# Moves between partitions, issued from two queues instead of one, in a fused attention and feed-forward kernel

## The chip, the core and the metric

The kernel runs on one core of a Trainium2 chip. The metric is the time of one execution on the device in microseconds (us), median of several runs. TensorE does matrix products, VectorE and ScalarE do elementwise work, GpSimd issues the loads here, and SyncE does nothing but issue transfers. Each engine takes its instructions in order. ScalarE can issue transfers as well, from the same in-order queue that holds its copies and exponentials.

## What is computed

The input is q, k and v of 8 batches, 8 heads, 576 positions and 64 features. Attention runs inside chunks of 64 positions; its output, 4608 tokens of 512 features, goes through a feed-forward part with a product in its middle:

```python
scores = scale * np.matmul(q_c, k_c.transpose(0, 1, 2, 4, 3))   # chunks of 64
attn = np.exp(scores - max) ; attn = attn / sum
x = np.matmul(attn, v_c)            # brought to [4608, 512]
a = x @ w1                          # [4608, 1024]
b = x @ w2
h = a * b @ w3
out = h @ w_out                     # [4608, 512], float32
```

The kernel works in bfloat16 with float32 accumulation and computes w3 @ w_out once, so that two products remain behind a * b.

## The kernel before

The whole schedule is a list of steps, ORDER, and each engine's instructions run in that order. The tokens are cut into 18 pairs of 256 tokens; two pairs form a group of 512. The letters that matter here:

- T transposes Q or K of a pair in blocks of 32 (VectorE). G moves the result of a group between partitions; S computes the scores (TensorE), E the exponential (ScalarE), P the product with V, N the normalisation (VectorE).
- X transposes the attention output (VectorE), H moves it between partitions.
- A and B are the two gate products of one slice (TensorE), C copies A's result from PSUM to SBUF (ScalarE), M multiplies it by B's (VectorE). A digit behind the dot is the slice; A8.4 is slice 4 of the group that begins with pair 8.
- O is the output product, Y its copy to SBUF (ScalarE), Q the store.

For pairs 0 to 7 neither G nor H is used: the scores are computed from blocks of 32 rows as they lie, and X writes the final layout. From pair 8 on, in groups 4 to 8, the 32-row blocks are moved so that scores need half as many matmuls. A move is a transfer from SBUF to SBUF, 32 partitions at a time.

```python
ps = ctx.enter_context(tc.tile_pool(name="ps", bufs=4, space=bass.MemoryType.PSUM))

def psum(name):                       # all PSUM tiles: four, in turn
    return ps.tile([P, 2, 512], f32, tag="p", name=name)

def move(dst, src):
    inorder(nc.sync.dma_start(dst, src))

def do_G(g, a):                       # a = 0 or 1: the two halves of the eight moves
    if a == 0:
        qkm_t[g] = asb.tile([P, 2, 2, 2, H, CH], bf, tag="qkm", bufs=2, name="qkm")
    for i in (0, 2, 1, 3):
        e = (i + a) % 2
        move(qkm_t[g][blk[i // 2 * 2 + e], i % 2], qkT_t[g][blk[i], e])

def do_H(g, a):
    xt = new_xt(g)[:].rearrange("p (s c) -> p s c", s=2)
    for i in (0, 2, 1, 3):
        move(xt[blk[i // 2 * 2 + a], i % 2], xm_t[g][blk[i], a].rearrange("p o m t -> p (o m t)"))

def do_C(p, j):
    a_t[p, j] = msb.tile([P, 512], f32, tag="a_sb", bufs=3, name="a_sb")
    inorder(nc.scalar.copy(a_t[p, j][:], ps_t[p, j][:, 0, :]))

def do_M(p, j):
    ...
    inorder(nc.vector.tensor_mul(o, view(a_t.pop((p, j))[:]), view(ps_t.pop((p, j))[:, 1, :])))

def store(p, u0, u1, n0, n1, o_sb):
    move(out[p * PT + u0 * UT:p * PT + u1 * UT, n0:n1].rearrange("(u p) n -> p u n", p=UT), o_sb)
```

Loads go through GpSimd's queue. The stretches of ORDER in which groups 5 and 6 are moved (cut):

```
... N8.0 A6.0 M4.7 B6.0 N8.1 C6.0 G5.1 A6.1 X8.0 B6.1 M6.0 C6.1 X8.1 P9 v15 q16 k16 A6.2 M6.1 ...
... C6.5 M6.4 A6.6 M6.5 B6.6 T12.1 H4.1 C6.6 S10 S11 M6.6 E10 A6.7 T13.0 B6.7 E11 P10 v16 q17 k17
T13.1 C6.7 O4 M6.7 G6.0 N10.0 N10.1 X10.0 G6.1 P11 v17 Y4 X10.1 O5 N11.0 N11.1 Q4 X11.0 X11.1 T14.0
A8.0 H5.0 Y5 B8.0 T14.1 C8.0 A8.1 M8.0 B8.1 H5.1 C8.1 T15.0 A8.2 B8.2 M8.1 C8.2 T15.1 Q5 A8.3 B8.3
C8.3 M8.2 G7.0 S12 M8.3 S13 E12 A8.4 T16.0 B8.4 E13 G7.1 P12 T16.1 C8.4 A8.5 B8.5 M8.4 ...
```

Of the kernel before, what the change touches and what calls it, by code (L numbers as in the profile page):

```python
# [7 lines left out]

ORDER = """
R0 R1 v0 q1 i0 k1 v1 i1 i2 q2 k2 v2 i3 q3 k3 v3 q4 k4 v4 o h0 h1 D0.0.16.64 K0 T0.0 K1 T0.1 q5 k5 v5  # L10
S0 T1.0 E0 P0 D0.1.4.512 T1.1 q6 k6 v6 N0.0 S1 D1.0.5.512 X0.0 N0.1 X0.1 A0.0 E1 B0.0 C0.0 P1 M0.0
A0.1 N1.0 X1.0 B0.1 C0.1 N1.1 A0.2 X1.1 B0.2 C0.2 M0.1 A1.0 T2.0 B1.0 C1.0 M0.2 A1.1 T2.1 q7 k7 v7
B1.1 C1.1 M1.0 S2 M1.1 A0.3 E2 T3.0 B0.3 C0.3 P2 M0.3 A1.2 N2.0 X2.0 B1.2 C1.2 N2.1 A1.3 X2.1 B1.3
C1.3 M1.2 A2.0 T3.1 q8 k8 v8 B2.0 C2.0 M1.3 S3 T4.0 A2.1 E3 M2.0 B2.1 T4.1 q9 k9 C2.1 P3 v9 M2.1
A2.2 N3.0 B2.2 C2.2 X3.0 A2.3 N3.1 B2.3 X3.1 C2.3 M2.2 S4 M2.3 A3.0 E4 B3.0 C3.0 A3.1 M3.0 B3.1 C3.1
V0 A3.2 M3.1 B3.2 C3.2 V1 A3.3 M3.2 B3.3 C3.3 V2 W0 M3.3 V3 W1 Z0 V4 V5 W2 Z1 V6 V7 T5.0 Z2 W3 T5.1
q10 k10 T6.0 T6.1 P4 v10 q11 k11 Z3 S5 N4.0 O0 E5 X4.0 N4.1 X4.1 T7.0 O1 T7.1 Y0 Q0 T8.0 P5 v11 q12
k12 Y1 S6 T8.1 O2 Q1 E6 N5.0 X5.0 N5.1 X5.1 O3 T9.0 T9.1 Y2 G4.0 P6 v12 q13 k13 A4.0 N6.0 B4.0 G4.1
Y3 X6.0 N6.1 C4.0 A4.1 X6.1 B4.1 C4.1 M4.0 Q2 S7 Q3 M4.1 A4.2 E7 T10.0 B4.2 C4.2 T10.1 P7 v13 q14
k14 A4.3 M4.2 B4.3 N7.0 C4.3 A4.4 X7.0 M4.3 B4.4 C4.4 N7.1 A4.5 M4.4 B4.5 C4.5 X7.1 S8 M4.5 S9 E8  # L20
A4.6 T11.0 B4.6 E9 T11.1 P8 v14 q15 k15 C4.6 A4.7 M4.6 G5.0 B4.7 C4.7 N8.0 A6.0 M4.7 B6.0 N8.1 C6.0
G5.1 A6.1 X8.0 B6.1 M6.0 C6.1 X8.1 P9 v15 q16 k16 A6.2 M6.1 N9.0 B6.2 C6.2 N9.1 A6.3 M6.2 B6.3 C6.3
X9.0 A6.4 M6.3 B6.4 C6.4 X9.1 A6.5 T12.0 H4.0 B6.5 C6.5 M6.4 A6.6 M6.5 B6.6 T12.1 H4.1 C6.6 S10 S11
M6.6 E10 A6.7 T13.0 B6.7 E11 P10 v16 q17 k17 T13.1 C6.7 O4 M6.7 G6.0 N10.0 N10.1 X10.0 G6.1 P11 v17
Y4 X10.1 O5 N11.0 N11.1 Q4 X11.0 X11.1 T14.0 A8.0 H5.0 Y5 B8.0 T14.1 C8.0 A8.1 M8.0 B8.1 H5.1 C8.1
T15.0 A8.2 B8.2 M8.1 C8.2 T15.1 Q5 A8.3 B8.3 C8.3 M8.2 G7.0 S12 M8.3 S13 E12 A8.4 T16.0 B8.4 E13
G7.1 P12 T16.1 C8.4 A8.5 B8.5 M8.4 C8.5 N12.0 A8.6 M8.5 B8.6 C8.6 N12.1 A8.7 M8.6 B8.7 C8.7 X12.0
P13 M8.7 A10.0 X12.1 B10.0 C10.0 N13.0 A10.1 M10.0 B10.1 N13.1 C10.1 A10.2 X13.0 B10.2 M10.1 C10.2
X13.1 S14 S15 M10.2 E14 A10.3 H6.0 T17.0 B10.3 E15 P14 T17.1 C10.3 A10.4 H6.1 M10.3 B10.4 C10.4
N14.0 A10.5 M10.4 B10.5 G8.0 C10.5 N14.1 A10.6 M10.5 B10.6 C10.6 X14.0 P15 G8.1 X14.1 A10.7 M10.6  # L30
B10.7 N15.0 C10.7 O6 N15.1 M10.7 X15.0 X15.1 H7.0 S16 Y6 S17 O7 E16 E17 H7.1 P16 Y7 O8 Q6 N16.0 Q7
N16.1 X16.0 X16.1 P17 Y8 A12.0 N17.0 Q8 B12.0 N17.1 C12.0 A12.1 X17.0 B12.1 M12.0 C12.1 X17.1 A12.2
M12.1 H8.0 B12.2 C12.2 A12.3 M12.2 B12.3 C12.3 H8.1 A12.4 M12.3 B12.4 C12.4 A12.5 M12.4 B12.5 C12.5
A12.6 M12.5 B12.6 C12.6 A12.7 M12.6 B12.7 C12.7 O9 M12.7 O10 Y9 Q9 A14.0 Y10 B14.0 C14.0 Q10 A14.1
M14.0 B14.1 C14.1 A14.2 M14.1 B14.2 C14.2 A14.3 M14.2 B14.3 C14.3 A14.4 M14.3 B14.4 C14.4 A14.5
M14.4 B14.5 C14.5 A14.6 M14.5 B14.6 C14.6 A14.7 M14.6 B14.7 C14.7 O11 M14.7 O12 Y11 Q11 A16.0 Y12
B16.0 C16.0 Q12 A16.1 M16.0 B16.1 C16.1 A16.2 M16.1 B16.2 C16.2 A16.3 M16.2 B16.3 C16.3 A16.4 M16.3
B16.4 C16.4 A16.5 M16.4 B16.5 C16.5 A16.6 M16.5 B16.6 C16.6 A16.7 M16.6 B16.7 C16.7 O13 M16.7 O14
Y13 Q13 O15 Y14 Q14 O16 Y15 Q15 Y16 Q16 O17
"""  # L40


# [1 line left out]
def kernel(  # L44
# [11 lines left out]
    nc = tc.nc  # L56
# [30 lines left out]
    def inorder(ins):  # L87
        tc.keep_in_program_order(ins)
        return ins

    def mm(*a, **kw):
        return inorder(nc.tensor.matmul(*a, **kw))  # L92
# [4 lines left out]
    def psum(name):  # L97
        return ps.tile([P, 2, 512], f32, tag="p", name=name)
# [74 lines left out]
    blk = [slice(i * BL, (i + 1) * BL) for i in range(NB)]  # L173
    qkT_t, qkm_t, s_t, e_t, pv_t, xn_t, xm_t, xt_t = {}, {}, {}, {}, {}, {}, {}, {}
# [1 line left out]

    def move(dst, src):
        inorder(nc.sync.dma_start(dst, src))  # L180

    def do_T(p, s, h=None):

# [8 lines left out]
    def do_G(g, a):  # L192

        if a == 0:
            qkm_t[g] = asb.tile([P, 2, 2, 2, H, CH], bf, tag="qkm", bufs=2, name="qkm")

        for i in (0, 2, 1, 3):
            e = (i + a) % 2
            move(qkm_t[g][blk[i // 2 * 2 + e], i % 2], qkT_t[g][blk[i], e])

    def do_S(p, hh=None):
        g, m = divmod(p, 2)
# [50 lines left out]
    def new_xt(g):  # L253

        if g not in xt_t:
            xt_t[g] = asb.tile([P, KO * GT], bf, tag="xt", bufs=4, name="xt")
        return xt_t[g]
# [18 lines left out]
    def do_H(g, a):  # L276

        xt = new_xt(g)[:].rearrange("p (s c) -> p s c", s=2)
        for i in (0, 2, 1, 3):
            move(xt[blk[i // 2 * 2 + a], i % 2], xm_t[g][blk[i], a].rearrange("p o m t -> p (o m t)"))  # L280

    ab_t, ps_t, a_t, o_t = {}, {}, {}, {}

    def do_D(which, p, n, cols):

        d, key = (s_t, p) if which == 0 else (ps_t, (p, 0))
        if key not in d:
            d[key] = psum("z_ps")
        for _ in range(n):
            mm(d[key][:, 0, 0:cols], lhsT=zero[:, 0:P], rhs=zero[:, 0:cols], start=True, stop=True)  # L290
# [43 lines left out]
    def store(p, u0, u1, n0, n1, o_sb):  # L334
        move(out[p * PT + u0 * UT:p * PT + u1 * UT, n0:n1].rearrange("(u p) n -> p u n", p=UT), o_sb)
# [63 lines left out]
    def load_half3(i):  # L399
# [7 lines left out]


    do = {"q": load_q, "k": load_k, "v": load_v, "i": load_w12, "o": load_wo, "h": load_half3, "T": do_T, "S": do_S, "R": do_R, "K": do_K, "E": do_E, "G": do_G, "H": do_H,
          "P": do_P, "N": do_N, "X": do_X, "A": do_A, "B": do_B, "C": do_C, "M": do_M, "D": do_D, "V": do_V,  # L410
          "W": do_W, "Z": do_Z, "O": do_O, "Y": do_Y, "Q": do_Q}
    for step in ORDER.split():
# [31 lines left out]
```

The softmax here doesn't subtract the row's maximum and nothing guards it: scores larger than these inputs give would overflow.

## Time and profile before

| | |
|---|---|
| time, median of 3 runs | 244.96 us (244.9 to 246.0) |
| span of the profiled execution | 244.5 us |
| transfers G (qkm<-qkT), issued by SyncE | 40, of 128 KB, 6.3 us from issue to landing (median) |
| transfers H (xt<-xm), issued by SyncE | 40, of 64 KB, 2.9 us |
| stores of the output, issued by SyncE | 20 |
| SyncE's hardware queue, its packets' time | 24.1% of 16 engines' span |
| GpSimd's software queue, its packets' time | 83.1% of 16 engines' span |

In the profile PE is TensorE, PEld its loading of weights, DVE VectorE, ACT ScalarE, POOL GpSimd and SP SyncE; "SPq" is SyncE's queue issuing a transfer, and the time shown for it is that of the issue, not of the data. The data's landing is a separate figure. Busy shares are averages over the span; what a change is worth is read from the stretch of time in which it acts, and from which wait ended last there. A view of waits names who waited, for whom, and how long in total.

### The profile page before, as it was taken

Reading aid. Unit: us, or ns where it says so; the run is one execution under the profiler, and the core shown is the slowest. Engines: PE = TensorE matmul, PEld = TensorE weight load, DVE = VectorE, ACT = ScalarE, POOL = GpSimd, SP = SyncE. Lnnn points to the kernel's source line nnn. Section 1 sums busy time; section 2 is a strip of 40 time slices with the busy share of each in tenths; the row PEclk is TensorE's granted clock in tenths of the full one; section 3 lists DMA queues with packets and bytes.
Section 4 is the critical chain, followed back from the end, with each engine's and each line's share of the span. In section 5 each row is a group of like instructions: output and inputs, shape, how many; then the busy total and the mean of one; then the engine's idle time right before and its main releaser. Section 6 shows DMA issues by size and latency. Waiting matters only on the chain.

```text
span 244.5 us, 6344 instructions
## 1 busy us (share of the span) xinstructions
PE 226.6 (93%) x2731; PEld 120.8 (49%) x2753; DVE 154.2 (63%) x232; ACT 85.2 (35%) x116; POOL 82.9 (34%) x110
## 2 busy tenths in 40 slices
PE   1279999999999999999998999999999999999994
PEld 1238777874445444444444444444444444444443
DVE  1675899698799588999997789918530232143000
ACT  2411423423233344425234335253231433332322
POOL 8847875556994346763740000000000000000000
PEclk9999999999999999999999999999999999999999
DMA  7999999999999999999999913735502200400244
GB/s 178 181 183 179 185 168 203 197 192 168 166 174 217 223 222 262 180 214 197 200 210 247 294 42 89 173 78 208 149 0 88 86 0 0 173 1 1 86 172 172
DMA packets 93595, 37.63 MB, mean 154 GB/s; under 512 B 75008, under 2 KB 86528, under 8 KB 93568
## 3 DMA queue, kind: packets, MB, share of 16 engines
q0 software_dynamic: 82592, 18.88, 83.1%
q1 hardware_dynamic: 9936, 17.83, 24.1%
q10 hardware_dynamic: 1040, 0.52, 0.8%
q8 instruction: 21, 0.34, 0.6%
q14 instruction: 6, 0.05, 0.1%
HBM read 38.80 MB, written 9.44 MB: 197 GB/s over the span
## 4 chain that ended last, share of the span: by engine, by line
PE 78%; DMA 8%; DVE 6%; SPq 3%; issue 2%; POOL 2%; ACT 1%; DVEq 0%; POOLq 0%
PE ab_ps L92 43%; PE o_ps L92 22%; PE w_ps L92 6%; DMA qkm<-qkT 5%; DMA qk<-in_k_dram 3%; PE s_ps L92 3%; SPq L180 3%; PE pv L92 2%; PE z_ps L92 2%; DVE qkT L188 2%; DVE xt L263 1%; DVE xn L251 1%; DVE ab L332 1%; POOL vbuf L95 1%; ACT a_sb L317 1%
## 5 line engine op out<-in xcount | busy, mean ns | idle before, releaser
L92 PE MATMUL ab_ps<-xt,w 128*128 128x512 bf16 (+1 forms) x681 | 126.8, 342 | 1.1 <-DVE xt L263 0.6
L92 PEld LDWEIGHTS <-w 128*128 128x128 bf16 x704 | 67.4, 98 | 55.2 <-DVE xt L263 1.2
L332 DVE TENSOR_TENSOR ab<-a_sb,ab_ps 128x512 bf16<-128x512 f32 x71 | 47.9, 676 | 45.0 <-ACT a_sb L317 44.9
L317 ACT COPY a_sb<-ab_ps 128x512 f32<-128x512 f32 x71 | 41.6, 586 | 81.0 <-PE ab_ps L92 79.1
L92 PE MATMUL o_ps<-w3o,ab 128*128 128x512 bf16 (+1 forms) x285 | 63.3, 373 | 0.6
L188 DVE STREAM_TRANSPOSE qkT<-qk 128x1024 bf16<-128x1024 bf16 x36 | 45.1, 1289 | 9.2 <-ACT qk L139 5.5
L92 PEld LDWEIGHTS <-ab 128*128 128x128 bf16 x296 | 28.5, 98 | 32.3
L95 POOL DMA_DIRECT2D vbuf<-in_v_dram x40 | 33.9, 856 | 20.9 <-DMA qk<-in_q_dram 6.4
L362 ACT COPY o_sb<-o_ps 128x1024 f32<-128x1024 f32 x17 | 17.2, 1012 | 44.8 <-PE o_ps L92 41.3
L251 DVE TENSOR_TENSOR xn<-pv,rc 128x512 bf16<-128x512 f32 x36 | 24.9, 691 | 1.2
L95 POOL DMA_DIRECT2D qk<-in_k_dram x23 | 18.0, 784 | 9.1 <-DMA vbuf<-in_v_dram 6.2
L95 POOL DMA_DIRECT2D qk<-in_q_dram x23 | 18.2, 793 | 6.9 <-DMA qk<-in_k_dram 1.5
L221 ACT ACTIVATE e<-s_ps 128x1024 bf16<-128x1024 f32 x16 | 15.9, 1026 | 3.4 <-PE s_ps L92 3.3
L92 PE MATMUL w_ps<-wo,w3T 128*128 128x512 bf16 x62 | 13.9, 379 | 0.1
L271 DVE STREAM_TRANSPOSE xm<-xn 128x512 bf16<-128x512 bf16 x20 | 13.6, 697 | 0.2
L248 DVE RECIPROCAL rc<-pv 128x8 f32<-128x8 f32 x36 | 6.9, 191 | 10.5 <-PE pv L92 10.5
L95 POOL DMA_DIRECT2D w<-in_moe_w_dram x16 | 11.1, 697 | 4.5 <-DMA wo<-in_moe_w_out_dram 1.5
L92 PEld LDWEIGHTS <-e 64*32 64x32 bf16 (+1 forms) x832 | 7.9, 97 | 7.9 <-issue 6.1
L263 DVE STREAM_TRANSPOSE xt<-xn 128x512 bf16<-128x512 bf16 x16 | 11.4, 711 | 0.5
L92 PEld LDWEIGHTS <-qkT 32*64 32x64 bf16 x512 | 5.7, 117 | 11.3 <-DVE qkT L188 9.6
L92 PE MATMUL pv<-vbuf,e 64*32 64x65 bf16 (+1 forms) x832 | 10.1, 198 | 1.1 <-ACT e L221 1.1
L355 DVE COPY o_sb<-o_ps 128x256 f32<-128x256 f32 x1 | 0.4, 425 | 16.0 <-PE o_ps L92 16.0
(23 smaller groups left out, 53.9 us busy)
## 6 DMA issues: line engine op xcount, KB each, us to landing
out_dram<-o_sb SPq DMA_DIRECT2D x17, 512.0 KB, 3.5
qkm<-qkT SPq DMA_DIRECT2D x40, 128.0 KB, 6.3
vbuf<-in_v_dram POOLq DMA_DIRECT2D x32, 128.0 KB, 8.7
w<-in_moe_w_dram POOLq DMA_DIRECT2D x16, 256.0 KB, 9.6
qk<-in_q_dram POOLq DMA_DIRECT2D x11, 256.0 KB, 7.6
qk<-in_k_dram POOLq DMA_DIRECT2D x11, 256.0 KB, 9.2
xt<-xm SPq DMA_DIRECT2D x40, 64.0 KB, 2.9
wo<-in_moe_w_out_dram POOLq DMA_DIRECT2D x4, 256.0 KB, 6.9
```

Source lines behind the costliest of these rows:

```text
L92: return inorder(nc.tensor.matmul(*a, **kw))
L95: return inorder(nc.gpsimd.dma_start(dst, src))
L180: inorder(nc.sync.dma_start(dst, src))
L188: inorder(nc.vector.transpose(qkT_t[g][:, :, p % 2, s, heads(h)].rearrange("p e h (y t) -> p h t e y", t=2), qk_t[p][:, s, heads(h)].rearr ...
L221: inorder(nc.scalar.activation(e_t[p][:, :, heads(hh)], s_t[p][:].rearrange("p u (h q) -> p u h q", q=CH)[:, :, heads(hh)], Exp, scale=sca ...
L248: inorder(nc.vector.reciprocal(rc[:], pv[:, :, :, D:W]))
L251: inorder(nc.vector.tensor_mul(xn_t[p][:, u], pv[:, :, :, 0:D], rc.to_broadcast([P, 2, 4, D])))
L263: inorder(nc.vector.transpose(new_xt(g)[:].rearrange("p (o t) -> p o t", o=KO)[:, :, t0:t0 + UT] .rearrange("p o (m y) -> p m o y", y=BL), ...
L271: inorder(nc.vector.transpose(xm_t[g][:, u, :, m].rearrange("p o (c y) -> p c o y", y=BL), xn_t[p][:].rearrange("p u r m d -> p (u r) m d" ...
L317: inorder(nc.scalar.copy(a_t[p, j][:], ps_t[p, j][:, 0, :]))
L332: inorder(nc.vector.tensor_mul(o, view(a_t.pop((p, j))[:]), view(ps_t.pop((p, j))[:, 1, :])))
L362: inorder(nc.scalar.copy(o_sb[:], ps_t.pop(p)[:]))
```

## The change

The second half of each G and of each H (a = 1) is issued by ScalarE's queue instead of SyncE's. It is meant to let the eight moves of a step go out from two queues side by side, so that their issue no longer stands in one line with the stores. No transfer is added or removed, and sizes and the order of the steps are as before.

```diff
-    def move(dst, src):
-        inorder(nc.sync.dma_start(dst, src))
+    def move(dst, src, eng=None):
+        inorder((eng or nc.sync).dma_start(dst, src))
 ...
-            move(qkm_t[g][blk[i // 2 * 2 + e], i % 2], qkT_t[g][blk[i], e])
+            move(qkm_t[g][blk[i // 2 * 2 + e], i % 2], qkT_t[g][blk[i], e], (nc.sync, nc.scalar)[a])
 ...
-            move(xt[blk[i // 2 * 2 + a], i % 2], xm_t[g][blk[i], a].rearrange("p o m t -> p (o m t)"))
+            move(xt[blk[i // 2 * 2 + a], i % 2], xm_t[g][blk[i], a].rearrange("p o m t -> p (o m t)"),
+                 (nc.sync, nc.scalar)[a])
 ...
-    def do_D(which, p, n, cols):
-        d, key = (s_t, p) if which == 0 else (ps_t, (p, 0))
+    def do_D(which, p, j, n, cols):
+        d, key = ((s_t, p), (ps_t, (p, j)), (pv_t, (p, 0)))[which]
```

The last part gives the dummy matmuls at the start (D) one more argument; the three D steps of ORDER are rewritten for it (D0.0.16.64 becomes D0.0.0.16.64, and so on) and do what they did.

More of the change, by code (lines that the diff above doesn't have):

```diff
@@ L9 @@
 ORDER = """
[L10 to L36, printed above, removed]
@@ L37 @@
-B16.0 C16.0 Q12 A16.1 M16.0 B16.1 C16.1 A16.2 M16.1 B16.2 C16.2 A16.3 M16.2 B16.3 C16.3 A16.4 M16.3
-B16.4 C16.4 A16.5 M16.4 B16.5 C16.5 A16.6 M16.5 B16.6 C16.6 A16.7 M16.6 B16.7 C16.7 O13 M16.7 O14
-Y13 Q13 O15 Y14 Q14 O16 Y15 Q15 Y16 Q16 O17
+R0 R1 v0 q1 i0 k1 v1 i1 i2 q2 k2 v2 i3 q3 k3 v3 q4 k4 v4 o h0 h1 D0.0.0.16.64 K0 T0.0 K1 T0.1 q5 k5
+v5 S0 T1.0 E0 P0 D0.1.0.4.512 T1.1 q6 k6 v6 N0.0 S1 D1.0.0.5.512 X0.0 N0.1 X0.1 A0.0 E1 B0.0 C0.0 P1
+M0.0 A0.1 N1.0 X1.0 B0.1 C0.1 N1.1 A0.2 X1.1 B0.2 C0.2 M0.1 A1.0 T2.0 B1.0 C1.0 M0.2 A1.1 T2.1 q7 k7
@@ new lines @@
+v7 B1.1 C1.1 M1.0 S2 M1.1 A0.3 E2 T3.0 B0.3 C0.3 P2 M0.3 A1.2 N2.0 X2.0 B1.2 C1.2 N2.1 A1.3 X2.1
+B1.3 C1.3 M1.2 A2.0 T3.1 q8 k8 v8 B2.0 C2.0 M1.3 S3 T4.0 A2.1 E3 M2.0 B2.1 T4.1 q9 k9 C2.1 P3 v9
+M2.1 A2.2 N3.0 B2.2 C2.2 X3.0 A2.3 N3.1 B2.3 X3.1 C2.3 M2.2 S4 M2.3 A3.0 E4 B3.0 C3.0 A3.1 M3.0 B3.1
+C3.1 V0 A3.2 M3.1 B3.2 C3.2 V1 A3.3 M3.2 B3.3 C3.3 V2 W0 M3.3 V3 W1 Z0 V4 V5 W2 Z1 V6 V7 T5.0 Z2 W3
+T5.1 q10 k10 T6.0 T6.1 P4 v10 q11 k11 Z3 S5 N4.0 O0 E5 X4.0 N4.1 X4.1 T7.0 O1 T7.1 Y0 Q0 T8.0 P5 v11
@@ new lines @@
+q12 k12 Y1 S6 T8.1 O2 Q1 E6 N5.0 X5.0 N5.1 X5.1 O3 T9.0 T9.1 Y2 G4.0 P6 v12 q13 k13 A4.0 N6.0 B4.0
+G4.1 Y3 X6.0 N6.1 C4.0 A4.1 X6.1 B4.1 C4.1 M4.0 Q2 S7 Q3 M4.1 A4.2 E7 T10.0 B4.2 C4.2 T10.1 P7 v13
+q14 k14 A4.3 M4.2 B4.3 N7.0 C4.3 A4.4 X7.0 M4.3 B4.4 C4.4 N7.1 A4.5 M4.4 B4.5 C4.5 X7.1 S8 M4.5 S9
+E8 A4.6 T11.0 B4.6 E9 T11.1 P8 v14 q15 k15 C4.6 A4.7 M4.6 G5.0 B4.7 C4.7 N8.0 A6.0 M4.7 B6.0 N8.1
+C6.0 G5.1 A6.1 X8.0 B6.1 M6.0 C6.1 X8.1 P9 v15 q16 k16 A6.2 M6.1 N9.0 B6.2 C6.2 N9.1 A6.3 M6.2 B6.3
@@ new lines @@
+C6.3 X9.0 A6.4 M6.3 B6.4 C6.4 X9.1 A6.5 T12.0 H4.0 B6.5 C6.5 M6.4 A6.6 M6.5 B6.6 T12.1 H4.1 C6.6 S10
+S11 M6.6 E10 A6.7 T13.0 B6.7 E11 P10 v16 q17 k17 T13.1 C6.7 O4 M6.7 G6.0 N10.0 N10.1 X10.0 G6.1 P11
+v17 Y4 X10.1 O5 N11.0 N11.1 Q4 X11.0 X11.1 T14.0 A8.0 H5.0 Y5 B8.0 T14.1 C8.0 A8.1 M8.0 B8.1 H5.1
+C8.1 T15.0 A8.2 B8.2 M8.1 C8.2 T15.1 Q5 A8.3 B8.3 C8.3 M8.2 G7.0 S12 M8.3 S13 E12 A8.4 T16.0 B8.4
+E13 G7.1 P12 T16.1 C8.4 A8.5 B8.5 M8.4 C8.5 N12.0 A8.6 M8.5 B8.6 C8.6 N12.1 A8.7 M8.6 B8.7 C8.7
+X12.0 P13 M8.7 A10.0 X12.1 B10.0 C10.0 N13.0 A10.1 M10.0 B10.1 N13.1 C10.1 A10.2 X13.0 B10.2 M10.1
@@ new lines @@
+C10.2 X13.1 S14 S15 M10.2 E14 A10.3 H6.0 T17.0 B10.3 E15 P14 T17.1 C10.3 A10.4 H6.1 M10.3 B10.4
+C10.4 N14.0 A10.5 M10.4 B10.5 G8.0 C10.5 N14.1 A10.6 M10.5 B10.6 C10.6 X14.0 P15 G8.1 X14.1 A10.7
+M10.6 B10.7 N15.0 C10.7 O6 N15.1 M10.7 X15.0 X15.1 H7.0 S16 Y6 S17 O7 E16 E17 H7.1 P16 Y7 O8 Q6
+N16.0 Q7 N16.1 X16.0 X16.1 P17 Y8 A12.0 N17.0 Q8 B12.0 N17.1 C12.0 A12.1 X17.0 B12.1 M12.0 C12.1
+X17.1 A12.2 M12.1 H8.0 B12.2 C12.2 A12.3 M12.2 B12.3 C12.3 H8.1 A12.4 M12.3 B12.4 C12.4 A12.5 M12.4
+B12.5 C12.5 A12.6 M12.5 B12.6 C12.6 A12.7 M12.6 B12.7 C12.7 O9 M12.7 O10 Y9 Q9 A14.0 Y10 B14.0 C14.0
@@ L40 @@
+Q10 A14.1 M14.0 B14.1 C14.1 A14.2 M14.1 B14.2 C14.2 A14.3 M14.2 B14.3 C14.3 A14.4 M14.3 B14.4 C14.4
+A14.5 M14.4 B14.5 C14.5 A14.6 M14.5 B14.6 C14.6 A14.7 M14.6 B14.7 C14.7 O11 M14.7 O12 Y11 Q11 A16.0
+Y12 B16.0 C16.0 Q12 A16.1 M16.0 B16.1 C16.1 A16.2 M16.1 B16.2 C16.2 A16.3 M16.2 B16.3 C16.3 A16.4
+M16.3 B16.4 C16.4 A16.5 M16.4 B16.5 C16.5 A16.6 M16.5 B16.6 C16.6 A16.7 M16.6 B16.7 C16.7 O13 M16.7
+O14 Y13 Q13 O15 Y14 Q14 O16 Y15 Q15 Y16 Q16 O17
 """
```

## Prediction

> **What bounds the kernel now.** I read the page's busy line, then busy time by stage, then the waits engine by engine, then the timelines of the three queues that the change touches. First the page's busy line (us, share of the span, instructions):
>
> ```profile
> PE 226.6 (93%) x2731; PEld 120.8 (49%) x2753; DVE 154.2 (63%) x232; ACT 85.2 (35%) x116; POOL 82.9 (34%) x110
> ```
>
> Then rows of the table by stretches (columns: the stretch and its length in us, busy time of PE, PEld, DVE, ACT and POOL with counts, granted clock, DMA share, GB/s):
>
> ```profile
> 0.00:20.00 20.00, 9.04 (x229) 6.01 (x232) 8.75 (x17) 5.32 (x5) 14.08 (x22) 1.00 1.44 182
> ...
> 110.00:120.00 10.00, 9.89 (x145) 4.64 (x148) 9.50 (x14) 4.19 (x6) 5.17 (x7) 1.00 1.85 200
> 120.00:130.00 10.00, 9.95 (x76) 4.67 (x78) 9.90 (x15) 3.79 (x5) 4.68 (x6) 1.00 1.59 216
> 130.00:140.00 10.00, 8.97 (x131) 4.39 (x130) 7.37 (x12) 4.28 (x6) 0.00 (x0) 1.00 1.43 273
> ```
>
> TensorE is the bound. Of its 18 us of idle time 11 lie in the first 20 us, before any move, and 3 behind its last matmul, which ends at 241.2. In between it is 94% busy or more in every stretch, mostly 99, except from 130 to 140, where 1.0 us is missing. The chain of 128x512 matmuls confirms that busy is real work here: 64 of them take 13.81 us, 216 ns each. VectorE is as full as TensorE from 110 to 130 us. ScalarE is a third busy.
>
> What do the moves cost TensorE? A line of its own waits over the whole run (who waited for whom: us in total, times, longest):
>
> ```profile
> PE s_ps L92 <- DMA qkm<-qkT: 1.0, 1, 1.0
> ```
>
> And the waits of SyncE's queue between 124 and 135 us, in the same columns:
>
> ```profile
> SPq L180 <- DMA qkm<-qkT: 2.7, 2, 1.9
> SPq L180 <- DVE ab L332: 1.6, 1, 1.6
> SPq L180 <- DMA out_dram<-o_sb: 0.9, 1, 0.9
> ```
>
> TensorE waits for a move once in the whole run, 1.03 us at 130.97, for the qkm of pair 12. The chain of waits charges 4.6% to that DMA and 2.9% to SyncE's queue, but TensorE worked beside nearly all of it. **The most that the change can give is thus about 1.0 us.** SyncE's lines show what I take to be the risk: moves wait for earlier moves. In the trace the hardware-queue transfers use eight semaphores in turn (108, 109, 112 to 117), and each waits until the transfer eight places before it has landed. The two first loads, one on SyncE and one on ScalarE, take 108 and 109: the turn is one for both queues.
>
> [...] The trace has no stretch with moves from two queues; it does show that issue is what there is to save, 0.59 us each in SyncE's queue. [...] the next issue starts some 45 ns after the last ended. [...] the semaphore instruction behind a ScalarE copy always starts 6 to 7 ns after that copy starts (85.537 and 85.544), never while the copy still waits. I take it that a move behind a copy is issued beside the copy's execution, but not before the copy's own wait has ended.
>
> **The change, part by part.** G moves the transposed Q and K of a group of two pairs, H the attention output of one; each issues eight moves in two halves (G5.0, G5.1), and the second half of four goes to ScalarE. With groups 4 to 8 that is 2 x 5 x 4 = 40 of 80 moves. The order of the steps is the same, and the dummy matmul's extra argument changes nothing. Removed from SyncE: 40 x 0.63 us = 25 us of a queue that mostly waits. Added to ScalarE: ten blocks of four, each about 4 x 0.59 + 3 x 0.045 = 2.5 us if nothing is waited for. In a stretch of gate matmuls ScalarE's copies start every 1.73 us, as its timeline shows (start, duration, operation, in brackets the idle time before it):
>
> ```profile
> 102.76 0.59 ACT L317 COPY a_sb<-ab_ps 128x512 f32<-128x512 f32 x1 [1.14 <-PE ab_ps L92]
> 104.48 0.59 ACT L317 COPY a_sb<-ab_ps 128x512 f32<-128x512 f32 x1 [1.14 <-PE ab_ps L92]
> 106.70 0.59 ACT L317 COPY a_sb<-ab_ps 128x512 f32<-128x512 f32 x1 [1.62 <-PE ab_ps L92]
> ```
>
> And SyncE's timeline where its queue is fullest:
>
> ```profile
> 117.43 6.37 SPq L180 DMA_DIRECT2D qkm<-qkT  x8
> 123.89 0.59 SPq L180 DMA_DIRECT2D out_dram<-o_sb  x1
> 124.58 9.41 SPq L180 DMA_DIRECT2D xt<-xm  x8
> ```
>
> A block issued from a copy's start holds the next copy for about 2.5 + 0.05 - 1.73 = 0.8 us. Whether that reaches TensorE depends on PSUM: four buffers, so a tile waits for the fourth tile before it. I walk through the ten.
>
> G4.1: ready at 80.84, ScalarE idle until 83.12; the next copy is 0.3 us late and is not needed so early. Cost 0.
> G5.1: behind the copy at 102.76, done 105.3. The next copy slips 0.85, its multiply ends 106.65 instead of 105.8. That multiply frees the tile A6.3 needs at 106.49. Cost about 0.25.
> H4.1: behind the copy at 111.88. The next copy, both exponentials and their tiles slip 0.85 against TensorE's stream; O4 at 116.35 needs the second exponential, which ended at 116.03, and had 0.32 to spare. Cost about 0.55. Sum 0.8. VectorE, without slack here, starts all that follows some 1 us later.
> G6.1: waits for its transpose (about 118.4) and for H4.1 to land (its last move begun at about 114.2, and such moves took 5.9 to 6.9 us). Issued by about 121.3 instead of 122.8, beside G6.0. The pair-12 scores no longer wait: gain 1.0. The next copy, Y4, slips half a microsecond, harmless.
> H5.1: behind the copy at 125.68 + 0.8 = 126.5. Its four moves wait, in ScalarE's own queue, for the landings of G6.1's last three and of the store Q4. In this stretch landings take 5 to 9.7 us for qkm and 9.6 for the store, so: G6.1 from 127 to 130.5, Q4 (issued about 122.5) up to 132. ScalarE is stuck until R, somewhere from 130.5 to 133. Behind R come one copy (0.59), one multiply (0.69), a 1.28 us transpose and another multiply (0.65) before A8.4 gets its buffer: R + 3.15. A8.4 began at 132.86. R = 130.5 puts the total shift at +0.8, R = 133.2 at +3.5; at R = 131.8 it is +2.1, the gain of 1.0 included.
> G7.1: waits likewise for H5.1 and the store Q5. ScalarE can catch up while TensorE stalls, but if those land at 138 to 138.5 a copy due at 137 is late by 1.5, with about 0.65 to spare. 0 to 1.5, say 0.5.
> H6.1, G8.1, H7.1, H8.1: loads have ended, landings take 1.9 to 3.3 us, so no block waits for one. H6.1 and G8.1 hold a copy by 0.35, H8.1 by 0.85 in a pure gate stretch where a tile has 3.6 us to spare. Cost 0. The store Q7 goes out earlier, but the end is TensorE's stream.
>
> Sum at the middle: 2.1 + 0.5 = +2.6 us.
>
> **The rivals.** First: landings get quicker because moves are spread over two queues, R falls below 129.7, H5.1 costs nothing, and what is left is 0.25 + 0.55 - 1.03, about -0.2: no change. For it: SyncE's H5 takes 9.41 us just because one queue carries all. Against it: POOL's loads keep the DMA engines nine tenths busy in every slice of the page up to 140 us, and they decide the landing, not the issuer. I give it one in four. Second: the trace's stalls on ScalarE are worse, as each late copy delays VectorE, which is full from 110 to 130 and holds the transposes for later moves; stalls then add up to 5 or 6 us, 250 us or a bit over. One in eight. Third: SyncE's queue was a hidden bound and freeing it pulls in all later work. Against it: TensorE's only move wait is 1.03 us; the best time this allows is about 243.9. One in ten. A fourth, that issues in two queues at once slow each other: the two first loads overlap at 0.73 us and take 0.43 and 0.48, no slower than others; and most blocks here follow each other anyhow.
>
> **Range and chances.** The rival of no loss at one quarter and +2.6 at three quarters give +1.95, so 246.9 us. The range runs from a small gain, 244.3, to the stacked stalls, 250.2. Two per cent is 4.9 us: faster by that is impossible by the waits (0.01), slower by it needs nearly twice my sum (0.11).
>
> **What would show it.** ScalarE's queue should have ten groups of four moves, with H5.1 spread over 4 to 6 us and waiting for qkm or the store; the copies after G5.1, H4.1 late by 0.8; TensorE waiting for VectorE's ab or ScalarE's e near 106, 116 and 131 to 137 us, and no longer for qkm at 131. After 165 us the two streams should be equal but for the shift. If ScalarE's issues pass waiting copies, or landings drop below 5 us at 118 to 132, the loss goes away and my number is too high; if the semaphores turn separately for each queue, R loses its wait for Q4 and the same holds.

## The result and the profile after

The changed kernel takes 256.84 us (median; 256.5 to 257.84), the kernel before, beside it, 245.07: a ratio of 1.048, interval 1.0438 to 1.0519. The prediction was 246.9 with 250.2 as its upper end. Spreading the moves over two queues cost 11.8 us.

The profile page of the changed kernel, busy time of the engines:

```profile
PE 232.0 (91%) x2731; PEld 122.3 (48%) x2753; DVE 153.5 (60%) x232; ACT 84.8 (33%) x116; POOL 82.7 (32%) x110
```

The counts are those of before, so no work was added. VectorE and ScalarE are no busier, but TensorE is busy 5.4 us longer with the same matmuls, and idle for some 6 us more. The table by stretches shows where (the columns are those of the table in the prediction):

```profile
90.00:100.00 10.00, 7.95 (x89) 3.35 (x90) 6.02 (x10) 2.36 (x4) 5.07 (x7) 0.83 1.78 223
...
130.00:140.00 10.00, 6.88 (x63) 3.10 (x61) 4.62 (x6) 2.47 (x5) 0.00 (x0) 1.00 1.22 220
140.00:150.00 10.00, 8.59 (x88) 3.71 (x88) 7.16 (x12) 3.35 (x5) 0.00 (x0) 0.66 0.55 147
```

There are two places, not one: 2 us of TensorE's time missing at 90 to 100, and 4.5 us at 130 to 150. The granted clock, the first figure behind POOL's count, falls with both: 0.83 over 10 us is 3.4 us at half clock, 0.66 is 6.8 us. What TensorE waited for between 85 and 160 us (who for whom: us in total, times, longest):

```profile
PE ab_ps L92 <- DVE ab L333: 3.3, 2, 2.0
PE s_ps L92 <- DVE ab L333: 3.2, 1, 3.2
PE s_ps L92 <- issue: 1.1, 1, 1.1
PE o_ps L92 <- ACT e L221: 0.4, 1, 0.4
```

The wait for qkm (1.03 us in before) is gone. In its place stand three waits for VectorE's multiply, 6.5 us in all. TensorE's timeline of the changed kernel shows them in brackets, with what follows each:

```profile
95.83 5.30 PE L92 MATMUL ab_ps<-xt,w 128*128 128x512 bf16 x16 [2.00 <-DVE ab L333]
...
140.12 0.49 PE L92 MATMUL s_ps<-qkm 64*64 64x64 bf16 x32 [3.25 <-DVE ab L333]
141.90 3.57 PE L92 MATMUL ab_ps<-xt,w 128*128 128x512 bf16 x8 [1.28 <-DVE ab L333]
```

Eight matmuls take 3.57 us at the last line. The same eight in before, at full clock:

```profile
132.86 1.90 PE L92 MATMUL ab_ps<-xt,w 128*128 128x512 bf16 x8
```

VectorE is only the messenger. Its own timeline ahead of the first stall:

```profile
88.22 0.69 DVE L333 TENSOR_TENSOR ab<-a_sb,ab_ps 128x512 bf16<-128x512 f32 x1 [0.60 <-ACT a_sb L318]
92.74 2.48 DVE L188 STREAM_TRANSPOSE qkT<-qk 128x1024 bf16<-128x1024 bf16 x2 [3.84 <-DMA vbuf<-in_v_dram]
```

The step that waits 3.84 us is T10.0, the transpose of pair 10's Q. In before it began without such a wait:

```profile
88.61 2.50 DVE L188 STREAM_TRANSPOSE qkT<-qk 128x1024 bf16<-128x1024 bf16 x2
```

T10.0 does not read V, so the releaser named in the bracket cannot be what it needed; experiment 2 finds what was. For the later stalls, ScalarE's timeline:

```profile
123.31 3.51 ACTq L180 DMA_DIRECT2D qkm<-qkT  x4
126.86 1.01 ACT L363 COPY o_sb<-o_ps 128x1024 f32<-128x1024 f32 x1 [4.39 <-DVE xm L271]
...
131.42 0.58 ACT L318 COPY a_sb<-ab_ps 128x512 f32<-128x512 f32 x1 [0.77 <-PE ab_ps L92]
132.89 5.78 ACTq L180 DMA_DIRECT2D xt<-xm  x4
138.77 1.56 ACT L318 COPY a_sb<-ab_ps 128x512 f32<-128x512 f32 x3 [6.77 <-DMA xt<-xm]
```

The line at 132.89 is H5.1: four issues that take 5.78 us instead of 2.5, and ScalarE does nothing else from 132.0 to 138.77. Behind them stand three copies, which then run in one go. SyncE's timeline of the same stretch:

```profile
123.34 3.01 SPq L180 DMA_DIRECT2D qkm<-qkT  x4
128.00 0.38 SPq L180 DMA_DIRECT2D out_dram<-o_sb  x1
129.29 5.30 SPq L180 DMA_DIRECT2D xt<-xm  x4
```

Read the two together with the semaphores in the trace. The first move of G6.1 is issued at 123.31, with semaphore 116, and lands at 127.94. The store Q4, eight places later and with semaphore 116 again, is issued at 128.00. It lands at 138.13. The last move of H5.1, eight places after Q4 and with semaphore 116 too, is issued at 138.16. ScalarE thus waited for a store that had waited for a move. Did the landings themselves get quicker over two queues? From the page (issuer, count, KB, median us from issue to landing):

```profile
qkm<-qkT SPq DMA_DIRECT2D x20, 128.0 KB, 5.9
qkm<-qkT ACTq DMA_DIRECT2D x20, 128.0 KB, 8.1
```

No: over those of these moves whose landing the trace has in full (35 of 40) the shortest, median and longest are 2.3, 7.0 and 9.1 us, and were 2.3, 6.3 and 9.7 in before.

### The profile page after: what moved, and what is told of

Read it like the earlier page. It is cut to its first block, busy times and chain, and to the rows that moved or that the text cites. A ratio compares the mean times of both kernels' runs of the same rounds, so it can differ in the third digit from the quotient of the medians.

```text
span 256.1 us, 6337 instructions
## 1 busy us (share of the span) xinstructions
PE 232.0 (91%) x2731; PEld 122.3 (48%) x2753; DVE 153.5 (60%) x232; ACT 84.8 (33%) x116; POOL 82.7 (32%) x110
## 4 chain that ended last, share of the span: by engine, by line
PE 70%; DMA 12%; DVE 9%; issue 2%; POOL 2%; ACT 1%; ACTq 1%; SPq 1%; DVEq 0%; POOLq 0%
PE ab_ps L92 40%; PE o_ps L92 19%; DMA qkm<-qkT 5%; PE w_ps L92 5%; DMA out_dram<-o_sb 4%; DVE qkT L188 4%; DMA qk<-in_k_dram 3%; PE z_ps L92 2%; PE s_ps L92 2%; DVE xn L251 2%; PE pv L92 2%; DVE xt L263 2%; DVE ab L333 2%; ACT a_sb L318 1%; ACTq L180 1%
## 5 line engine op out<-in xcount | busy, mean ns | idle before, releaser
L92 PE MATMUL ab_ps<-xt,w 128*128 128x512 bf16 (+1 forms) x681 | 131.1, 349 | 4.5 <-DVE ab L333 3.3
L92 PEld LDWEIGHTS <-w 128*128 128x128 bf16 x704 | 68.8, 100 | 62.3 <-issue 9.5
L248 DVE RECIPROCAL rc<-pv 128x8 f32<-128x8 f32 x36 | 6.9, 191 | 10.2 <-PE pv L92 10.2
L374 DVE STREAM_TRANSPOSE w3T<-w 128x1024 bf16<-128x1024 bf16 x8 | 9.7, 1231 | 1.0 <-PE w_ps L92 1.0
```

The source lines that it names most:

```text
L248: inorder(nc.vector.reciprocal(rc[:], pv[:, :, :, D:W]))
L374: inorder(nc.vector.transpose(w3T_t[f][:].rearrange("p k (f y) -> p f k y", y=BL), w3[:, NB * f:NB * (f + 1), :].rearrange("p f (k x) -> p ...
```

## The experiments

Each was timed beside the kernel before on its chip; ratios are to that. "Shift" is how much later an instruction starts than in the trace of before. In the expectations e1 to e9 are the experiments 1 to 9.

**1. The buffers as they were.** The built programs hold one difference that the diff doesn't show. The transposed Q and K of a group share two buffers. In before, group 5 gets that of group 3; in the changed kernel it gets that of group 4, whose moves have just been issued. Here the buffers are fixed as in before; all else is the changed kernel.

```diff
-    qkT_t[g] = asb.tile([...], bf, tag="qkT", bufs=2, name="qkT")
+    qkT_t[g] = asb.tile([...], bf, tag=f"qkT{g % 2}", bufs=1, name="qkT")
```

> The changed kernel, with the transposed Q and K (qkT) of group g held in buffer g mod 2, as in the kernel before. Theory A: about 4.5 of the 11.8 us come from the build having put group 5 into group 4's buffer, so that pair 10's transpose waited for all eight moves of group 4. With the old placement that wait and the halved TensorE clock behind it go: 252.0 us (251 to 253), and TensorE runs on at 94 us. Rival (the wait came from loads slowed by two move queues): no change, 256 to 257. The wait of the gate stretch near 130 us stays in both.

Measured: 254.09 us, ratio 1.035 (1.0295 to 1.0405). That is 1.3% less than the changed kernel, 3 us, where 4.8 were expected; the time lies outside the expected range. TensorE's waits between 85 and 165 us:

```profile
PE s_ps L92 <- DVE ab L333: 3.7, 1, 3.7
PE ab_ps L92 <- DVE ab L333: 1.4, 2, 1.1
```

The stall of 2.0 us at 94 is gone and T10.0 starts at 89.03. The later stalls stay, H5.1 even a little longer (6.84 us). The cause is real, and it isn't the larger one: without it 3.5 of the 4.8% remain.

**2. The kernel before with the changed kernel's buffers.** All moves on SyncE; only the placement is taken over.

```diff
-    tag="qkT", bufs=2
+    tag=f"qkT{(0, 1, 0, 1, 0, 0, 1, 0, 1)[g]}", bufs=1
```

> The kernel before, all moves on SyncE, with qkT in the buffers that the changed kernel got (group 5 in group 4's). Theory A: the same stall at pair 10 appears without any move on ScalarE, as group 4's moves land near 92.5 us here too: 249 us (248 to 250.5). Rival (it takes the second queue): 245.

Measured: 250.25 us, ratio 1.022 (1.0157 to 1.0282), as the theory expected. The profiled execution took 252.67, with a mean clock of 0.984, against 250.1 to 250.4 and 0.993 in the three others. VectorE's timeline:

```profile
94.06 2.46 DVE L188 STREAM_TRANSPOSE qkT<-qk 128x1024 bf16<-128x1024 bf16 x2 [5.16 <-DMA vbuf<-in_v_dram]
```

The placement alone makes T10.0 5.5 us late, with no move on ScalarE, and the bracket again names the load of V. In the changed kernel's trace VectorE executes four semaphore waits between 89.37 and 92.74, two semaphores each, and these are the eight of G4's moves: the transpose may not overwrite group 4's data before they have landed. The view names the event that came last before the start, which was a load's. So this part of the loss has nothing to do with ScalarE's queue. It comes from which buffer the build gave to group 5; why it chose another one isn't shown.

**3. H5.1 back on SyncE** (on top of 1).

```diff
-    (nc.sync, nc.scalar)[a])                  # in do_H
+    (nc.sync, nc.scalar)[a if g != 5 else 0])
```

> e1 with the second half of group 5's H back on SyncE, the other 36 moves stay on ScalarE. Theory B: most of what is left is that these four moves wait inside ScalarE's queue for earlier transfers to land and hold the gate copies behind them: about 4.5 us less than e1, 247.0 us (246 to 248.5), with no halved clock near 140 us. Rival (issue time on ScalarE, spread over all ten blocks, 0.5 us each): 0.5 us less than e1.

Measured: 253.14 us, ratio 1.0328 (1.0271 to 1.0386). Missed by 6 us: hardly better than 1. ScalarE's timeline says why:

```profile
134.47 5.46 ACTq L180 DMA_DIRECT2D qkm<-qkT  x4
140.03 1.07 ACT L318 COPY a_sb<-ab_ps 128x512 f32<-128x512 f32 x2 [5.43 <-DMA qkm<-qkT]
```

H5.1 is gone, and G7.1, the next block, waits in its stead (5.46 us, against 2.75 in 1). Its four moves wait for semaphores 109, 113, 115 and 117, again the transfers eight places earlier. The shift is +1.37 before the block and +7.03 at the end.

**4. The store Q4 behind H5.1** (on top of 1). If H5.1 waits for Q4 alone, this frees it.

```diff
- ... N11.1 Q4 X11.0 X11.1 ... M8.0 B8.1 H5.1 C8.1 ...
+ ... N11.1 X11.0 X11.1 ... M8.0 B8.1 H5.1 Q4 C8.1 ...
```

> e1 with the store Q4 put behind H5.1 in the list of steps, all moves stay on ScalarE. Q4 was the transfer that the last move of H5.1 waited for (138.16 us, 3.6 us behind the third). Theory B: ScalarE comes free some 3 us earlier, the time falls by 2.5 to 4 us against e1: 248.8 us (247.5 to 250). Rival (issue time): no change against e1.

Measured: 253.41 us, ratio 1.032 (1.0272 to 1.0369). Missed. ScalarE's timeline:

```profile
129.10 5.39 ACTq L181 DMA_DIRECT2D xt<-xm  x4
134.59 1.56 ACT L319 COPY a_sb<-ab_ps 128x512 f32<-128x512 f32 x3 [7.28 <-DMA xt<-xm]
```

With the store out of the way the third move waits for H5.0's first, issued at 125.12 and landed at 133.3. The theory that named one guilty transfer fell. Taken alone, 3 and 4 would speak for the rival, a loss by issue time, since both came out within 1 us of experiment 1; experiment 5 tells the two apart. In this stretch landings take about 8 us, and the trace has eight semaphores in turn, so about one transfer can be issued per us, whatever stands in the queue (an estimate from these two numbers; in the changed kernel 17 were issued in the 14.9 us from 123.31 to 138.16).

**5. H5.1 and G7.1 both on SyncE** (on top of 1). If two adjacent blocks take the wait in turns, both have to go; 32 moves stay on ScalarE.

```diff
-    (nc.sync, nc.scalar)[a])                              # in do_G
+    (nc.sync, nc.scalar)[a if g in (4, 5, 6, 8) else 0])
-    (nc.sync, nc.scalar)[a])                              # in do_H
+    (nc.sync, nc.scalar)[a if g in (4, 6, 7, 8) else 0])
```

> e1 with both H5.1 and G7.1 back on SyncE; the other 32 moves stay on ScalarE. In e3 only H5.1 went back and ScalarE then sat 5.5 us in G7.1, each of whose moves waited for a transfer eight places earlier to land. Theory B (ScalarE pays only where a block meets landings of 5 to 10 us): with both gone the loss is gone, 245.5 us (244.5 to 246.5), 8.5 us less than e1, although 32 issues of 0.6 us stay on ScalarE. Rival (issue time on ScalarE): 1 us less than e1, 253. Second rival (the wait moves on to the next block, H6.1): 249 to 252.

Measured: 246.32 us, ratio 1.0034 (1.0015 to 1.0054). Confirmed, and both rivals (253, and 249 to 252) are out. TensorE's waits between 85 and 165 us, all of them:

```profile
PE s_ps L92 <- issue: 1.1, 1, 1.1
PE o_ps L92 <- ACT e L221: 0.5, 1, 0.5
PE ab_ps L92 <- DMA qkm<-qkT: 0.2, 1, 0.2
```

No wait for a multiply is left, and the mean clock is 0.999. From 1 to 5 the loss falls by 3.2%: two blocks, eight of the 40 moves, cost that.

**6. The same two blocks on ScalarE, but later in its order** (on top of 1). H5.1 goes behind E13, G7.1 behind C8.7.

```diff
- ... B8.1 H5.1 C8.1 ... B8.4 E13 G7.1 P12 ... C8.7 X12.0 ...
+ ... B8.1 C8.1 ... B8.4 E13 H5.1 P12 ... C8.7 G7.1 X12.0 ...
```

> e1 with all 40 moves on ScalarE, but H5.1 put behind E13 and G7.1 behind C8.7 in the list of steps, so that they are issued when the earlier transfers have landed. Theory B: ScalarE no longer holds copies, the time falls to 246.5 us (245 to 249; the later data may hold A10 at 141 us for 1 to 2 us). Rival (issue time): no change against e1, 254.

Measured: 249.22 us, ratio 1.0135 (1.0077 to 1.0193); the range held it, the middle missed by 2.7. ScalarE's timeline:

```profile
134.38 3.16 ACTq L180 DMA_DIRECT2D xt<-xm  x4
137.64 1.07 ACT L318 COPY a_sb<-ab_ps 128x512 f32<-128x512 f32 x2 [3.95 <-DMA out_dram<-o_sb]
```

H5.1, 6 us later, takes 3.16 us instead of 6.84. G7.1 at 144.39 takes 2.44, so it waits for nothing. Being later helps as far as the landings are over, no further. The four executions fall in two pairs, 250.1 and 250.34 us at a mean clock of 0.993, and 247.9 and 248.34 at 0.998 and 1.000, so the median lies between the two.

**7. Only G6.1 on ScalarE** (buffers as in 1). The one block by which the wait for qkm was to vanish.

```diff
-    (nc.sync, nc.scalar)[a])                     # in do_G
+    (nc.sync, nc.scalar)[a if g in (6,) else 0])
-    (nc.sync, nc.scalar)[a])                     # in do_H
+    (nc.sync, nc.scalar)[a if g in () else 0])
```

> The kernel before (with its placement of qkT) and four moves alone on ScalarE: G6.1, the block that took TensorE's single wait for a move, 1.03 us at 131 us. Theory: that wait goes and nothing else is lost, 244.2 us (243.8 to 245.2), a ratio of 0.996. Rival (ScalarE, waiting in G6.1 for H4 to land, delays Y4 and what follows): 245.5 to 247.

Measured: 244.95 us, ratio 0.9965 (0.9946 to 0.9984): faster than both kernels. TensorE's only wait between 85 and 165 us:

```profile
PE s_ps L92 <- issue: 0.6, 1, 0.6
```

The shift at the end is -0.96 us, nearly the whole 1.03 that the prediction took as the most that could be gained.

**8. The changed kernel with H5.1 and G7.1 on SyncE** (its own buffers). The edit is that of 5, without that of 1; it shows whether the two causes add up.

> The changed kernel as it is, its own placement of qkT kept, with H5.1 and G7.1 back on SyncE. If the two causes add, what is left is the placement's: e2's 4.6 us over the kernel before, plus e5's 0.5: 250.5 us (249 to 252). Rival (they are one loss, the stall at pair 10 makes the later one): 253 or more; or the rest vanishes too: 247.

Measured: 248.96 us, ratio 1.0185 (1.0132 to 1.0238), just under the range that was expected. TensorE's waits between 85 and 165 us:

```profile
PE ab_ps L92 <- DVE ab L333: 2.8, 2, 2.3
```

The stall behind T10.0 remains, and the later ones are gone. The placement costs 1.3% with the two blocks on ScalarE (the changed kernel against 1) and 1.5% without them (8 against 5); the two blocks cost 2.9% with its placement and 3.2% with that of before. So the two causes add, and what they leave is the 0.3% of experiment 5. Each of these differences is uncertain by 0.6 to 0.7.

**9. Only H5.1 and G7.1 on ScalarE** (buffers as in 1): eight moves instead of 40.

```diff
-    (nc.sync, nc.scalar)[a])                     # in do_G
+    (nc.sync, nc.scalar)[a if g in (7,) else 0])
-    (nc.sync, nc.scalar)[a])                     # in do_H
+    (nc.sync, nc.scalar)[a if g in (5,) else 0])
```

> The placement of the kernel before, with only H5.1 and G7.1 on ScalarE, eight moves of the 80, all others on SyncE. Theory B: these eight alone bring nearly the whole loss of e1, 252 us (250 to 254), with ScalarE waiting in H5.1 for landings. Rival (issue time, by the number of moves): a fifth of e1's loss, 247.

Measured: 254.07 us, ratio 1.0374 (1.034 to 1.0408), just over the upper end of the range. Eight moves cost as much as the 40 of experiment 1. But the wait isn't in H5.1, where it was expected. ScalarE's timeline:

```profile
125.46 2.50 ACTq L180 DMA_DIRECT2D xt<-xm  x4
...
133.39 7.98 ACTq L180 DMA_DIRECT2D qkm<-qkT  x4
141.47 1.07 ACT L318 COPY a_sb<-ab_ps 128x512 f32<-128x512 f32 x2 [8.22 <-DMA qkm<-qkT]
```

H5.1 takes its bare 2.50 us and G7.1 waits 7.98, with a stall of 7.27 us on TensorE. With 3, where G7.1 waited 5.46, this settles the mechanism: which block waits depends on how the landings fall, but in each of these runs one of the two waited.

## Where the prediction was right and where it was wrong

Shifts of the changed kernel, step by step, in the profiled execution (257.84 us, mean clock 0.980; the three others, 256.5 to 257.05 us, had 0.986 to 0.987, so by an estimate from these shares they lack some 3.3 us of its 10.2 us at half clock):

| step | predicted, us | measured, us |
|---|---|---|
| start of the kernel | 0 | 0.33 |
| scores of pair 7, a wait whose end the view doesn't explain | not in the sum | 0.6 |
| buffer of group 5 | not in the sum | 3.8, of which 1.8 half clock |
| G5.1 | 0.25 | 0.26 |
| H4.1 | 0.55 | 0.6 |
| H5.1, with the gain of 1.0 | 1.3 | 5.8, of which 2.5 half clock |
| G7.1 | 0.5 | 0 |
| G4.1, H6.1, G8.1, H7.1, H8.1 | 0 | 0.1 |
| sum | 2.6 | 11.6 |

**The missing term.** "The order of the steps is the same, and the dummy matmul's extra argument changes nothing." The order is the same; the buffers are not. The prediction took it for granted that nothing else moves because nothing else stood in the diff. Experiments 1, 2 and 8 put 1.3 to 2.2% on this term. In the trace its 3.8 us are a stall of 2.00 and 1.84 of half clock (16 matmuls in 5.30 us, at 216 ns they take 3.46). The 0.6 us before it isn't the buffer's. It is a wait of TensorE at 88.09, 1.14 us long against 0.50 in before; experiments 1 and 5, where T10.0 doesn't wait for moves, have it too (0.88 and 1.05 us), and what ends it isn't shown. Added to the predicted 246.9, the 1.3 to 2.2% (3.2 to 5.4 us) lead to 250.1 to 252.3, at or past the upper end of the range by this term alone. The terms that follow were enough as well: experiment 1, without this one, took 254.09.

**The mis-sized term.** "R, somewhere from 130.5 to 133." The wait was right: H5.1's four moves waited for just what was named, G6.1's last three moves and the store Q4. The way from R to TensorE was right too: R + 3.15 was to be the start of A8.4. In the changed kernel H5.1's last issue ends at 138.67 (132.89 + 5.78), and A8.4 starts at 141.90, 3.23 later; in experiment 1 it is 134.93 and 138.16. But R itself came 2.0 to 2.4 us later than the middle of 131.8: taken back by the shift that the prediction did not have (4.9 us, 0.7 in experiment 1), it is 133.8 and 134.2. The failing input was the store, "Q4 (issued about 122.5) up to 132". Taken back in the same way, it was issued at 123.1 and landed at 133.2; in experiment 1 it is 125.3 and 133.7. The last move's issue then adds 0.5. At 122.47, in before, Q4's forerunner had landed, which was G6.0's first move. In the changed kernel the forerunner is G6.1's first move, which landed at 127.94, and at 125.94 in experiment 1. The chain was followed one link back where it had two. Experiment 4 shows that a better value for Q4 alone would not have saved the estimate, and 3, 5 and 9 show that the unit to be priced was the stretch of long landings, not one block. The 0.5 for G7.1 was of the wrong kind too: zero when H5.1 has taken the wait, 5.5 to 8 us of issue when it hasn't.

**The second missing term.** A stall was priced at its length, but the granted clock was 0.50 behind both stalls of the changed kernel: for 3.41 us from 96.01 on and for 6.83 us from 140.38 on. A8.4 starts with a shift of 9.04, and the end stands at 11.6: the difference is matmuls at half clock, at the same work and with no wait. In experiment 1 it is 5.31 and 7.54. The length of the stall alone does not tell whether this follows. Behind the stall of 2.00 us in the changed kernel 16 matmuls take 5.30 us. Behind the one of 2.31 us in experiment 8 they take 3.61, and that execution has a mean clock of 1.000. What decides it isn't shown.

**What was right.** TensorE was the bound, and its one wait for a move was the most to be gained (experiment 7). A block of four takes 2.5 us where nothing is waited for (2.46 in H4.1). ScalarE's later work did not pass a waiting issue: in H5.1 the copies stood behind it for 5.78 us. (In before, the semaphore instruction behind a copy starts 5 to 24 ns after it in 70 of 76 cases and 0.3 to 4.5 us after it in six, not always 6 to 7 ns, but never ahead of it.) The semaphores are one turn for both queues: H5.1's last move, on ScalarE, has the 116 of Q4, on SyncE. The stretches after 165 us are equal but for the shift. The prediction looked for a saving in issue time alone, and the landings of these moves got no quicker (median 6.3 us in before, 7.0 in the changed kernel). What the change moved was the issue's waiting. In before SyncE bore it (9.41 us for H5's eight moves), with nothing behind it but other transfers.

**The rivals.** The first (quicker landings, one in four) is false by the landings shown above. The second (stacked stalls, "250 us or a bit over", one in eight) had the right mechanism and was too small without the buffer and the clock. The third, SyncE as a hidden bound, is false: freeing it by 32 moves (experiment 5) made nothing faster. The fourth (issues in two queues slow each other) is small at most: side by side, G4.0 took 2.78 us on SyncE and G4.1 2.49 on ScalarE, and the first four of these moves took 2.51 in before.

**Open.** Neither shorter landings (fewer loads at the same time) nor more semaphores were tried. That a move waits for the transfer eight places earlier is read from the traces: in the changed kernel ten issues start 0.02 to 0.08 us after the landing of the transfer that last had their semaphore, and none of those whose landing the trace has in full starts before it. Why the start differs by some tenths of a us between these kernels isn't settled.

## What to carry to other kernels

Here an issue cost its queue not 0.6 us alone but also the time until the transfer that last had its semaphore had landed (5.78 us for the four issues of H5.1, 2.46 for those of H4.1). So move transfers to a compute engine's queue only where the earlier ones have landed, and price a stretch of slow landings as a whole: in experiment 3 the wait moved to the next block, where the four issues took 5.46 us. After any change of queues compare the buffers' addresses and the waits of untouched steps as well: here the build gave group 5 another buffer, and a wait of 3.84 us that named a transfer the step doesn't read was the sign of it. Look for the one block that ends a wait on the bound engine's path; here four moves gave what there was to gain and 40 lost 5%.

## What the runs showed of the hardware

In the changed kernel TensorE had half clock for 3.41 us from 96.01 on and for 6.83 us from 140.38 on. The mean clock of the profiled executions was 0.980 there, 0.984 in experiment 2, 0.986 in 1 and 3, 0.987 in 9, 0.991 in 4, 0.993 in 6, 0.999 in 5 and 1.000 in 7 and 8. It differs between executions of the same kernel: in experiment 8 one execution took 250.91 us at a mean clock of 0.993, the three others 248.8 to 249.1 at 0.999 to 1.000. In the changed kernel a move between partitions that was issued from 80 to 136 us, while loads ran (their last packet ended at 138.5), took 4.6 to 9.3 us to land and a store 7.9 to 10.1; after 145 us moves took 1.9 to 3.9. From 123.31 to 138.16 that delay, with eight semaphores in turn, and not the 0.6 us of issue set the rate of the queues: 17 issues in 14.9 us.
